# One pool of four two-bank PSUM tiles, and both halves of a block's bucket bits in one group, in a fused attention and channel-mix kernel

## The chip, the cores and the metric

The kernel runs on one core of one Trainium2 chip. Its measure is the device time in microseconds (us), the median of several executions. Executions of one kernel mostly agree within 1%. An execution more than 1.5% above the fastest of its kernel is called slow and is left out of every ratio.

## The reference, cut to what matters

```python
def _attn_ref(q, k, v, proj):                 # q, k, v: (4, 8, 768, 64); proj: (64, 6)
    q_bits = (np.einsum('bhsd,dk->bhsk', q, proj) > 0)
    k_bits = (np.einsum('bhsd,dk->bhsk', k, proj) > 0)
    # ... six bits make a bucket number ...
    mask = q_bucket[:, :, :, None] == k_bucket[:, :, None, :]
    scores = scale * np.matmul(q, k.transpose(0, 1, 3, 2))
    scores = np.where(mask, scores, -1000000000.0)
    # ... softmax ...
    return np.matmul(attn, v)

def _moe_ref(x, mu_k, mu_r, w_k, w_v, w_r):   # x: (4, 768, 512), heads side by side
    xk = mu_k * x + (1.0 - mu_k) * x_prev     # x_prev: x one row earlier
    xr = mu_r * x + (1.0 - mu_r) * x_prev
    k = np.maximum(xk @ w_k, 0.0)
    v = k * k @ w_v
    return 1.0 / (1.0 + np.exp(-(xr @ w_r))) * v
```

## The kernel before: the parts that matter

The kernel handles two heads at a time, as one of 16 blocks; four blocks make a batch, after which the "expert" matmuls (`w_k`, `w_r`, `w_v`) of that batch can run. The mask is built into the score matmul: each head's operands carry six extra rows with the signs of the projections. These signs come from the *bits* groups: matmuls on TensorE (PE), a VectorE (DVE) operation `bx` that reduces each result to a sign, and small copies into the operand's rows.

The program is recorded from a static plan. A list scheduler in the kernel file simulates the five engines with assumed durations and transfer times. At each free moment it takes the ready operation of lowest priority number (table `PR`). Then the instructions are recorded in exactly that order. On the chip every engine works through its own list in this order; semaphores, which the recording layer places, hold an instruction until what it depends on is done.

The kernel uses eight banks of PSUM, the memory that matmuls write to, of 512 fp32 columns each. Before, they were six tiles: two of two banks for score steps (1024 columns, read by one exp on ScalarE, ACT), and four of one bank for all small groups: bits, PV (the product of the exps with `v`), transposes, expert groups.

```python
    sc_t = [psum.tile([P, STEP], FP32, name=f"sc{i}", tag=f"sc{i}") for i in range(2)]
    sm_t = [psum.tile([P, 512], FP32, name=f"sm{i}", tag=f"sm{i}") for i in range(4)]
    plan = Plan({"sc": (2, 2), "sm": (4, 3)})     # slots; of them at most so many for expert groups
    # ...
    def sm(name):
        return sm_t[plan.slot[name]]
    # ... in add_bits, for each half h of the 768 columns:
            def f(nm=nm, h=h):
                ps = sm(nm)
                for w_, st in ((p1, True), (p2, False)):
                    for i in its:                 # q and k of both heads: four 32-row strips
                        a = side_a["qk"[i % 2]][sa]
                        nc.tensor.matmul(ps[32 * i : 32 * i + 32, 0:HALF], w_, a[:, i // 2, h * HALF : (h + 1) * HALF],
                                         start=st, stop=not st)
            def g(nm=nm, h=h):
                nc.vector.tensor_scalar(
                    out=bx_t[sx][lo_p:P, h * HALF : (h + 1) * HALF].bitcast(U16), # ...
                    scalar1=0x8000, scalar2=0x5400, op0=ALU.bitwise_and, op1=ALU.bitwise_or)
    # ... in the scheduler, when an operation takes a slot: the one that has been free longest
                    slot = avail[cls].pop(0)
```

The softmax here doesn't subtract the row's maximum and nothing guards it: scores larger than these inputs give would overflow.

Of the kernel before, what the change touches and what calls it, by code (L numbers as in the profile page):

```python
# [9 lines left out]
FP32 = mybir.dt.float32  # L10
FP16 = mybir.dt.float16
BF16 = mybir.dt.bfloat16
U16 = mybir.dt.uint16
AF = mybir.ActivationFunctionType
ALU = mybir.AluOpType
# [6 lines left out]


PR = {
    'ldq': -2.811, 'ldv': -2.337, 'hi': -5.393, 'lo': -1.084, 'tr': -2.122, 'bits': -1.224, 'bx': -4.393, 'row': 4.034,
    'va': 0.273, 'vsum': -2.003, 'mean': -0.515, 'pv0': 0.767, 'pv1': 1.128, 'fin': -1.916, 'ot': 1.215, 'xt': -1.326,
    'df': -1.607, 'xk': -3.487, 'xr': 2.133, 'moe': 4.97, 'mk': 2.095, 'mv': 2.279, 'sq': 0.189, 'os': 0.275,
    'tpe': -4.352, 'tev': -0.289, 'va_u': 2.059, 'vsum_u': -3.477, 'wk0': 38.237, 'wk1': 3.956, 'wr0': 54.984, 'wv0': 63.151,
    'wv1': -2.812, 'p0b': -9.506,
}  # L30


# [4 lines left out]
class Plan:  # L37
# [5 lines left out]



    def __init__(self, slots):
        self.ops = []
        self.writer = {}
        self.readers = {}
        self.slots = slots  # L50
        self.slot = {}

    def add(self, eng, dur, prio, fn, r=(), w=(), take=None, give=(), lag=None, name="", at=0.0, svc=0.0):
# [28 lines left out]
    def schedule(self):  # L82
        ops = self.ops
        engines = {"GQ": "POOL"}
        free = {e: 0.0 for e in ("PE", "ACT", "DVE", "POOL", "SP")}
        ready = {e: [] for e in free}
        avail = {c: list(range(n)) for c, (n, _) in self.slots.items()}
        moe_held = {c: 0 for c in self.slots}
        held = {}
        order = []  # L90
        events = [(o.at, 0, o.i) for o in ops]
        heapq.heapify(events)

        def met(i):
            o = ops[i]
            o.left -= 1
            if o.left == 0:
                heapq.heappush(ready[engines.get(o.eng, o.eng)], (o.prio, o.i))

        t = 0.0  # L100
        dma_free = 0.0
        while len(order) < len(ops):
            while events and events[0][0] <= t + 1e-9:
                _, kind, i = heapq.heappop(events)
                if kind == 0:
                    met(i)
                elif kind == 1:
                    o = ops[i]
                    for s in o.succ:
                        if ops[s].eng == o.eng and not o.svc:  # L110
                            met(s)
                elif kind == 2:
                    o = ops[i]
                    for s in o.succ:
                        if ops[s].eng != o.eng or o.svc:
                            met(s)
                    for name in o.give:
                        cls, slot, moe = held.pop(name)
                        avail[cls].append(slot)
                        moe_held[cls] -= moe  # L120
            progress = False
            for e in free:
                if free[e] > t + 1e-9:
                    continue
                skipped = []
                pick = None
                while ready[e]:
                    item = heapq.heappop(ready[e])
                    o = ops[item[1]]
                    if o.take is not None:  # L130
                        cls, name, moe = o.take
                        if not avail[cls] or (moe and moe_held[cls] >= self.slots[cls][1]):
                            skipped.append(item)
                            continue
                    if o.svc > 0.3 and o.prio > -9.0 and dma_free - t > BACKLOG:
                        skipped.append(item)
                        heapq.heappush(events, (dma_free - BACKLOG, 3, o.i))
                        continue
                    pick = o
                    break  # L140
                for item in skipped:
                    heapq.heappush(ready[e], item)
                if pick is None:
                    continue
                o = pick
                progress = True
                if o.take is not None:
                    cls, name, moe = o.take
                    slot = avail[cls].pop(0)
                    held[name] = (cls, slot, moe)  # L150
                    self.slot[name] = slot
                    moe_held[cls] += moe
                o.start = t
                free[e] = t + o.dur
                lag = o.lag
                if o.svc:
                    dma_free = max(t + o.dur + 0.9, dma_free) + o.svc
                    lag = max(lag, dma_free + 0.6 - t - o.dur)
                heapq.heappush(events, (t + o.dur + 0.1 * (o.eng in ("DVE", "ACT")), 1, o.i))
                o.vis = t + o.dur + lag  # L160
                heapq.heappush(events, (o.vis, 2, o.i))
                order.append(o)
            if not progress:
                if not events:
                    raise RuntimeError("the plan is stuck")
                t = max(t, events[0][0])
        self.end = max(o.start + o.dur for o in ops)
        return order
# [3 lines left out]
def kernel(  # L172
# [13 lines left out]
    nc = tc.nc  # L186

    B, H, S, D = q.shape
# [3 lines left out]
    P = 128  # L192
# [3 lines left out]
    HALF = S // 2  # L196
    STEP = 1024
# [26 lines left out]
    bx_t = [buf([P, S], FP16, f"bx{i}") for i in range(NBX)]  # L224
# [26 lines left out]
    p2 = buf([P, 32], FP16, "p2")  # L251
    muk = buf([P, NDC], FP32, "muk")
    mur = buf([P, NDC], FP32, "mur")
    sc_t = [psum.tile([P, STEP], FP32, name=f"sc{i}", tag=f"sc{i}") for i in range(2)]
    sm_t = [psum.tile([P, 512], FP32, name=f"sm{i}", tag=f"sm{i}") for i in range(4)]

    plan = Plan({"sc": (2, 2), "sm": (4, 3)})
    add = plan.add

    def sm(name):  # L260
        return sm_t[plan.slot[name]]

    DVE_C = lambda n, m=1.0: (n / m + 67) / 960.0
    ACT_C = lambda n: 0.068 + 0.833 * n / 1000.0
# [165 lines left out]
    def add_bits(n, heads):  # L430
        sa, sx = n % NAQ, n % NBX
        its = [2 * j + e for j in heads for e in range(2)]
        pb = n if n else PR["p0b"]
        lo_p = 64 * heads[0]
        for h in range(2):
            nm = f"bits{n}_{h}"

            def f(nm=nm, h=h):
                ps = sm(nm)
                for w_, st in ((p1, True), (p2, False)):  # L440
                    for i in its:
                        a = side_a["qk"[i % 2]][sa]
                        nc.tensor.matmul(ps[32 * i : 32 * i + 32, 0:HALF], w_, a[:, i // 2, h * HALF : (h + 1) * HALF],  # L443
                                         start=st, stop=not st)

            def g(nm=nm, h=h):
                nc.vector.tensor_scalar(  # L447
                    out=bx_t[sx][lo_p:P, h * HALF : (h + 1) * HALF].bitcast(U16),
                    in0=sm(nm)[lo_p:P, 0:HALF].bitcast(U16).rearrange("p (c e) -> p c e", e=2)[:, :, 1],
                    scalar1=0x8000, scalar2=0x5400, op0=ALU.bitwise_and, op1=ALU.bitwise_or)  # L450

            add("PE", 2 * MM(HALF) + 0.1, pb + PR["bits"], f, r=["p1", "p2"] + [("a", side, sa, j) for side in "qk" for j in heads],
                w=[(nm,)], take=("sm", nm, 0), name=nm)
            add("DVE", DVE_C(HALF), pb + PR["bx"], g, r=[(nm,)], w=[("bx", sx, h)], give=[nm], name=f"bx{n}")
        for i in its:
            side, j = "qk"[i % 2], i // 2

            def row(side=side, j=j, i=i):
                nc.sync.dma_start(out=side_a[side][sa][D : D + NB, j, :], in_=bx_t[sx][32 * i : 32 * i + NB, :])
            add("SP", 0.7, pb + PR["row"] + 0.01 * i, row, r=[("bx", sx, 0), ("bx", sx, 1)], w=[("ab", side, sa, j, h) for h in range(2)], svc=0.1, name=f"row{n}")  # L460

    def add_prep_first(n):
        s, sh, sa = n % NQ, n % NNH, n % NAQ
# [75 lines left out]
    def add_scores(n):  # L539
        sa, sp = n % NAQ, n % NPT  # L540
        for s in range(NSTEP):
# [4 lines left out]
            need += sorted({("ab", "k", sa, ch // NSC, (ch % NSC) // 3) for ch in chunks})  # L546

            def f(nm=nm, s=s):
                ps = sc_t[plan.slot[nm]]
                for lo, hi in pieces(s):  # L550
                    ch, q0 = divmod(lo, S)
                    j, jc = divmod(ch, NSC)
                    nc.tensor.matmul(ps[:, lo - s * STEP : hi - s * STEP], side_a["k"][sa][:, j, jc * P : (jc + 1) * P],  # L553
                                     side_a["q"][sa][:, j, q0 : q0 + hi - lo], start=True, stop=True)

            def g(nm=nm, s=s):
                nc.scalar.activation(out=pt_t[sp][:, s * STEP : (s + 1) * STEP], in_=sc_t[plan.slot[nm]],  # L557
                                     func=AF.Exp, bias=EBIAS, scale=ESC)

            T = n + s / NSTEP  # L560
# [187 lines left out]
```

## Time and profile before

| | |
|---|---|
| time, median of 3 | 258.73 us (258.31 to 258.94) |
| span in the profile | 256.8 us |
| PE / VectorE / ScalarE busy | 93% / 76% / 72% |

The head of the profile's page gives busy time, share of the span and number of instructions of each engine (PEld is PE's weight load):

```profile
span 256.8 us, 6319 instructions
## 1 busy us (share of the span) xinstructions
PE 239.3 (93%) x2519; PEld 143.5 (56%) x2519; DVE 195.1 (76%) x391; ACT 185.5 (72%) x242; POOL 57.9 (23%) x98
```

The table by stages gives, for each stretch of the span, each engine's busy us (number of instructions), then the granted PE clock, the DMA share and GB/s:

```profile
26.00:39.00 13.00, 12.04 (x188) 7.84 (x186) 9.07 (x18) 11.35 (x13) 4.11 (x7) 1.00 0.89 170
39.00:52.00 13.00, 10.92 (x155) 7.20 (x154) 9.52 (x18) 11.35 (x13) 2.85 (x7) 1.00 0.86 182
52.00:65.00 13.00, 11.04 (x149) 7.09 (x146) 9.80 (x18) 11.27 (x13) 7.60 (x13) 1.00 1.10 177
...
103.00:128.00 25.00, 25.00 (x303) 15.13 (x292) 23.05 (x44) 20.79 (x25) 6.48 (x8) 1.00 0.85 226
128.00:154.00 26.00, 24.90 (x283) 15.90 (x281) 24.50 (x52) 22.57 (x32) 8.63 (x11) 1.00 0.85 219
154.00:180.00 26.00, 26.00 (x274) 15.13 (x273) 23.52 (x43) 18.09 (x23) 5.64 (x8) 1.00 0.82 177
```

Before 65 us PE (first column of busy times) has gaps while ScalarE (fourth) is at 87%; later PE is full. The groups of instructions (busy us, mean ns of one, then idle time before them and its releaser):

```profile
L557 ACT ACTIVATE pt<-sc 128x1024 bf16<-128x1024 f32 x144 | 143.2, 1028 | 29.9 <-PE sc L553 28.3
...
L447 DVE TENSOR_SCALAR bx<-sm 128x384 uint16<-128x384 uint16 (+1 forms) x32 | 16.4, 549 | 3.3 <-PE sm L443 2.6
```

The table of waits (total us, times, longest) has these lines for the exps and scores, for the tanh of the `w_r` groups (`rs`), and for the multiply that follows it (`os`):

```profile
ACT pt L557 <- PE sc L553: 28.3, 48, 3.9
ACT rs L674 <- PE sm L671: 18.9, 13, 2.3
...
DVE os L688 <- PE sm L681: 16.4, 13, 2.1
...
PE sc L553 <- ACT pt L557: 4.5, 11, 0.7
```

Scores wait for a slot (last line), though only 4.5 us in all.

### The profile page before, as it was taken

Reading aid. Unit: us, or ns where it says so; the run is one execution under the profiler, and the core shown is the slowest. Engines: PE = TensorE matmul, PEld = TensorE weight load, DVE = VectorE, ACT = ScalarE, POOL = GpSimd, SP = SyncE. Lnnn points to the kernel's source line nnn. Section 1 sums busy time; section 2 is a strip of 40 time slices with the busy share of each in tenths; the row PEclk is TensorE's granted clock in tenths of the full one; section 3 lists DMA queues with packets and bytes.
Section 4 is the critical chain, followed back from the end, with each engine's and each line's share of the span. In section 5 each row is a group of like instructions: output and inputs, shape, how many; then the busy total and the mean of one; then the engine's idle time right before and its main releaser. Section 6 shows DMA issues by size and latency. Waiting matters only on the chain.

```text
span 256.8 us, 6319 instructions
## 1 busy us (share of the span) xinstructions
PE 239.3 (93%) x2519; PEld 143.5 (56%) x2519; DVE 195.1 (76%) x391; ACT 185.5 (72%) x242; POOL 57.9 (23%) x98
## 2 busy tenths in 40 slices
PE   6768898888999999999999989999999999999994
PEld 2334564555666456656666655555666666555441
DVE  4999676777789997989998999898685753675322
ACT  3838888888994598878898967586798986147320
POOL 2491415056051330504041424040000000000000
PEclk9998999999999999999999999999999999999999
DMA  6968979799998479796978987888200011220132
GB/s 191 382 168 155 163 174 172 199 171 180 225 201 227 116 199 175 212 241 190 274 148 266 216 241 149 233 164 166 89 3 6 3 41 43 82 86 1 41 123 82
DMA packets 64565, 39.78 MB, mean 155 GB/s; under 512 B 46756, under 2 KB 60952, under 8 KB 64536
## 3 DMA queue, kind: packets, MB, share of 16 engines
q1 hardware_dynamic: 62248, 36.76, 58.4%
q0 software_dynamic: 2208, 2.62, 6.3%
q8 instruction: 19, 0.31, 0.5%
q14 instruction: 10, 0.08, 0.1%
q10 hardware_dynamic: 80, 0.00, 0.0%
HBM read 24.12 MB, written 6.29 MB: 118 GB/s over the span
## 4 chain that ended last, share of the span: by engine, by line
PE 63%; DMA 15%; DVE 10%; POOL 3%; SPq 3%; issue 2%; ACT 2%; POOLq 0%; DVEq 0%
PE sc L553 16%; PE sm L681 15%; PE sm L652 11%; PE sm L583 10%; DMA vn<-in_v_dram 8%; PE sm L671 7%; PE sm L443 4%; DMA qn<-in_q_dram 3%; DMA ak<-kh 2%; POOL vt L360 2%; DMA kn<-in_k_dram 2%; PE sm L609 2%; ACT pt L557 2%; SPq L334 1%; DVE xk L635 1%
## 5 line engine op out<-in xcount | busy, mean ns | idle before, releaser
L557 ACT ACTIVATE pt<-sc 128x1024 bf16<-128x1024 f32 x144 | 143.2, 1028 | 29.9 <-PE sc L553 28.3
L553 PE MATMUL sc<-aq,ak 128*128 128x512 f16 (+1 forms) x384 | 84.6, 329 | 4.5 <-ACT pt L557 4.5
L553 PEld LDWEIGHTS <-ak 128*128 128x128 f16 x384 | 33.6, 98 | 31.1 <-issue 12.2
L652 PE MATMUL sm<-xk,wk 128*128 128x384 bf16 x256 | 48.9, 326 | 0.2
L681 PE MATMUL sm<-wv,k 128*128 128x512 bf16 x192 | 47.8, 379 | 1.1 <-DVE ob L599 1.1
L583 PEld LDWEIGHTS <-pt 128*128 128x128 bf16 x1152 | 42.9, 97 | 9.0 <-issue 0.6
L583 PE MATMUL sm<-va,pt 128*128 128x65 bf16 x1152 | 44.6, 193 | 0.0
L656 ACT ACTIVATE kr<-sm 128x384 bf16<-128x384 f32 x64 | 31.3, 498 | 9.5 <-PE sm L652 7.5
L652 PEld LDWEIGHTS <-wk 128*128 128x128 bf16 x256 | 24.1, 98 | 15.2 <-issue 0.3
L360 POOL TENSOR_TENSOR vt<-vn 128x384 f32<-128x384 f32 x12 | 15.1, 1256 | 71.5 <-DMA vn<-in_v_dram 71.5
L659 DVE TENSOR_TENSOR k<-kr 128x384 bf16<-128x384 bf16 x64 | 23.8, 385 | 8.5 <-ACT kr L656 8.4
L674 ACT ACTIVATE rs<-sm 128x512 f32<-128x512 f32 x24 | 14.4, 599 | 22.1 <-PE sm L671 18.9
L681 PEld LDWEIGHTS <-k 128*128 128x128 bf16 x192 | 18.4, 98 | 19.5 <-issue 1.3
L688 DVE SCALAR_TENSOR_TENSOR os<-rs,sm 128x512 f32<-128x512 f32 x24 | 16.3, 684 | 16.5 <-PE sm L681 16.4
L671 PE MATMUL sm<-wr,xr 128*128 128x512 bf16 x96 | 24.6, 379 | 0.0
L619 POOL COPY xt<-xt 128x127 bf16<-128x127 bf16 x16 | 8.4, 525 | 69.1 <-DVE xt L615 64.4
L447 DVE TENSOR_SCALAR bx<-sm 128x384 uint16<-128x384 uint16 (+1 forms) x32 | 16.4, 549 | 3.3 <-PE sm L443 2.6
L599 DVE TENSOR_TENSOR ob<-sm,rc 128x384 bf16<-128x384 f32 x32 | 17.8, 556 | 0.9
L405 DVE SCALAR_TENSOR_TENSOR kh<-kn,kh 128x768 f16<-128x768 f32 x15 | 18.3, 1219 | 0.1
L635 DVE SCALAR_TENSOR_TENSOR xk<-df,muk,xt 128x768 bf16<-128x768 bf16 x16 | 16.7, 1046 | 0.3
L443 PE MATMUL sm<-ak,p 128*32 128x384 f16 x124 | 14.4, 335 | 2.3 <-DVE ak L422 1.3
L635 DVE SCALAR_TENSOR_TENSOR xr<-df,mur,xt 128x768 bf16<-128x768 bf16 x16 | 16.1, 1018 | 0.0
(76 smaller groups left out, 195.3 us busy)
## 6 DMA issues: line engine op xcount, KB each, us to landing
vn<-in_v_dram SPq DMA_DIRECT2D x16, 384.0 KB
out_dram<-os SPq DMA_DIRECT2D x24, 256.0 KB
qn<-in_q_dram SPq DMA_DIRECT2D x15, 384.0 KB
kn<-in_k_dram SPq DMA_DIRECT2D x15, 384.0 KB
wk<-in_moe_w_k_dram POOLq DMA_DIRECT2D x4, 256.0 KB, 5.3
wv<-in_moe_w_v_dram POOLq DMA_DIRECT2D x4, 256.0 KB, 8.7
wr<-in_moe_w_r_dram POOLq DMA_DIRECT2D x2, 256.0 KB, 5.4
aq<-bx SPq DMA_DIRECT2D x31, 9.0 KB
```

The lines of the kernel that those rows point to most:

```text
L360: nc.gpsimd.tensor_tensor(out=vt[:, :, :, 0:E], in0=src[:, :, 0:3, 0:E], in1=src[:, :, 3:6, 0:E], op=ALU.add)
L405: nc.vector.scalar_tensor_tensor(out=nh[:, :, D:P], in0=nat.rearrange("p j (c d) -> p (j c) d", d=D), scalar=QS, in1=nh[:, :, 0:D], op0=AL ...
L443: nc.tensor.matmul(ps[32 * i : 32 * i + 32, 0:HALF], w_, a[:, i // 2, h * HALF : (h + 1) * HALF], start=st, stop=not st)
L553: nc.tensor.matmul(ps[:, lo - s * STEP : hi - s * STEP], side_a["k"][sa][:, j, jc * P : (jc + 1) * P], side_a["q"][sa][:, j, q0 : q0 + hi ...
L557: nc.scalar.activation(out=pt_t[sp][:, s * STEP : (s + 1) * STEP], in_=sc_t[plan.slot[nm]], func=AF.Exp, bias=EBIAS, scale=ESC)
L583: nc.tensor.matmul(oo[:, ic * 65 : ic * 65 + 65], pt_t[sp][:, o : o + P], va_t[sa][:, j, jc, 0 : D + 1], start=(not uc and ic == 0 and jc ...
L635: nc.vector.scalar_tensor_tensor(out=dst[smx], in0=df_t[sd], scalar=mu[:, t : t + 1], in1=x, op0=ALU.mult, op1=ALU.add)
L652: nc.tensor.matmul(ps[:, 0:HALF], wk_sb[:, d, fc * P : (fc + 1) * P], xk_t[mx[d]][:, h * HALF : (h + 1) * HALF], start=(d == 0), stop=(d = ...
L656: nc.scalar.activation(out=kr_t[sk], in_=sm(nm)[:, 0:HALF], func=AF.Relu, scale=0.5 ** 0.5)
L659: nc.vector.tensor_tensor(out=k2_t[s2][:, h * HALF : (h + 1) * HALF], in0=kr_t[sk], in1=kr_t[sk], op=ALU.mult)
L671: nc.tensor.matmul(sm(nr), xr_t[mx[d]][:, c * P : (c + 1) * P], wr_sb[:, d, :], start=(d == 0), stop=(d == NDC - 1))
L681: nc.tensor.matmul(sm(nv), k2_t[(b * NFC + fc) % NK2][:, c * P : (c + 1) * P], wv_sb[:, fc, :], start=(fc == 0), stop=(fc == NFC - 1))
```

## The change

All eight banks become one pool of four two-bank tiles. A score step takes a whole tile of the first three, when both banks are free; small groups take single banks, from bank 7 down to 4, so that they share banks 4 and 5 with the third score slot. The intent is a third score step in flight. The bits of both halves become one group of 768 columns, which takes a score slot, and one VectorE operation in place of two. All priorities are new as well.

```diff
 PR = {
-    'ldq': -2.811, 'ldv': -2.337, 'hi': -5.393, 'lo': -1.084, 'tr': -2.122, 'bits': -1.224, 'bx': -4.393, 'row': 4.034,
+    'ldq': -4.096, 'ldv': -2.786, 'hi': -4.393, 'lo': -1.809, 'tr': -9.712, 'bits': -6.189, 'bx': -3.768, 'row': 6.869,
     ... (all the other entries too)
+        def room(take):
+            cls, _, moe = take
+            if count[cls] >= self.most[cls] or (moe and count["moe"] >= self.moe_most):
+                return None
+            if cls == "sc":
+                for i in self.pairs:
+                    if not used[2 * i] and not used[2 * i + 1]:
+                        return i, (2 * i, 2 * i + 1)
+                return None
+            for b in self.banks:
+                if not used[b]:
+                    return b, (b,)
+            return None
     ...
-    sc_t = [psum.tile([P, STEP], FP32, name=f"sc{i}", tag=f"sc{i}") for i in range(2)]
-    sm_t = [psum.tile([P, 512], FP32, name=f"sm{i}", tag=f"sm{i}") for i in range(4)]
-    plan = Plan({"sc": (2, 2), "sm": (4, 3)})
+    ps_t = [psum.tile([P, STEP], FP32, name=f"ps{i}", tag=f"ps{i}") for i in range(4)]
+    plan = Plan((0, 1, 2), (7, 6, 5, 4), {"sc": 3, "sm": 4}, 3)
     def sm(name):
-        return sm_t[plan.slot[name]]
+        b_ = plan.slot[name]
+        return ps_t[b_ // 2][:, (b_ % 2) * 512 : (b_ % 2) * 512 + 512]
     ... (bits)
+            ps = ps_t[plan.slot[nm]]
+            for w_, st in ((p1, True), (p2, False)):
+                for lo, hi in ((0, 512), (512, S)):
                     for i in its:
-                        nc.tensor.matmul(ps[32 * i : 32 * i + 32, 0:HALF], w_, a[:, i // 2, h * HALF : (h + 1) * HALF], ...)
+                        nc.tensor.matmul(ps[32 * i : 32 * i + 32, lo:hi], w_, a[:, i // 2, lo:hi], start=st, stop=not st)
     ... (one tensor_scalar over ps[lo_p:P, 0:S] in place of two over 0:HALF)
-                w=[(nm,)], take=("sm", nm, 0), name=nm)
+            w=[(nm,)], take=("sc", nm, 0), name=nm)
```

## The prediction

> **What bounds the kernel now.** Two regimes. The table by stages shows TensorE (PE) busy throughout from 103 us to 231 us (24.90 of 26 us at worst), and the chain of waits there is almost all matmuls. Costing matmuls at the densest spacing in the timeline (a score step 0.44 us, a third of a PV group 0.38, four expert matmuls 0.65 or 0.86, a block's bits 0.76), I estimate 227 us of dense PE work in a span of 256.8. From 77 us the PE has no idle time worth naming until the last matmul at 253 us. The loss lies before 65 us, where I estimate only 44 us of dense PE work. There ScalarE sets the pace: from 26 to 65 us it runs 38 exp steps, although nine in a row took 8.72 us (0.97 each), so 40 would fit. From 13 to 26 us it runs 8 where 13 would fit; one wait is 3.86 us (second head's scores, behind its bits, the VectorE operation and the row copies).
>
> The groups show exp waiting for scores 28.3 us over 48 waits, scores for exp 4.5 us over 11. Most lie after 77 us and cost nothing. From 30 to 66 us they are 0.2-1.0 us each: with two score slots, every burst of PV, bits or transposes on the PE delays the refill. Such regular bubbles can mean that PSUM has run out (the Trainium skill, Perfetto Trace Analysis, "Optimization Strategy"); the trace agrees: score matmuls wait 0.32 us for an exp.
>
> **What the change does.**
> - A third score slot when two small banks are free, as they mostly are before 65 us. It lets exp run through a PE burst: I expect 2-3.5 us of ScalarE idle gone. In expert stages it is often missing; nothing is lost.
> - The bits group holds a score slot for about 2 us (matmuls, wait, VectorE): costs perhaps 0.5 us of the above.
> - Bits matmuls: 16 either way, same columns: still about 0.76 us a block.
> - VectorE: two operations of 549 ns become one of 768 columns. At 1.04 ns a column on about 150 ns fixed (from 549 at 384) that is 0.95 us: 0.15 us less a block, 2.3 us in all, perhaps 0.3 us of it critical at the start. Against it: it starts only after all 16 matmuls, so first bits matmul to row copies (1.6 us now) grows by 0.2-0.3 us. Nearly cancel.
> - New priorities (transposes of block 1 and bits earlier, xr far later) can move the start by 1-2 us either way; I count -0.5.
>
> A us saved on ScalarE before the PE saturates moves the end by one us; later, nothing. Sum: -3 to -3.5 us. The tail (expert matmuls from 228 us) stays.
>
> **Predicted: 255.4 us, 8 in 10 between 251.0 and 258.9.** Faster by over 2%: 0.24; within 2%: 0.70; slower: 0.06.
>
> **What would show it.** Right: 2-4 more exps before 65 us; most gaps of 0.2-0.6 us there gone; first expert matmuls 2-4 us earlier; PE full until 4 us before the end; the VectorE operation 0.95 us x16, its matmuls unchanged. Wrong: the same exp count by 65 us, or exp waiting while bits hold a slot.
>
> **What would make it wrong.** The start (before 26 us) improving by several us through the order, which would give over 2%; late xr stalling the r groups and emptying the PE; bits holding slots at bad moments.

## The result, and the profile after

| | before | after |
|---|---|---|
| time, median | 258.60 us (258.31 to 258.94) | 291.72 us (290.83 to 295.62) |
| ratio, 95% interval | | 1.1255 (1.1215 to 1.1295) |
| PE / VectorE / ScalarE busy | 93% / 76% / 72% | 86% / 67% / 64% |
| exp steps begun in the first 65 us | 45 | 40 |
| first expert matmul | 63.4 us | 68.9 us |

The change made the kernel 33 us slower. (The median before is now of four executions, one more than above.) The exps are counted once each, where they begin. The table by stages counts an exp that crosses a border in both stages; so the 38 exps that the prediction reads from it for 26 to 65 us are 35 that begin there, and there was more room than it says. The head of the page, the table by stages (the same columns as above), and the groups:

```profile
span 289.6 us, 6322 instructions
## 1 busy us (share of the span) xinstructions
PE 250.0 (86%) x2519; PEld 147.0 (51%) x2519; DVE 192.9 (67%) x375; ACT 184.8 (64%) x242; POOL 56.4 (19%) x98
```

```profile
26.00:39.00 13.00, 11.83 (x182) 7.63 (x181) 9.82 (x16) 11.20 (x12) 4.77 (x6) 1.00 0.82 131
39.00:52.00 13.00, 8.73 (x113) 5.81 (x110) 6.88 (x12) 8.96 (x10) 2.97 (x5) 0.91 0.68 164
52.00:65.00 13.00, 11.12 (x140) 7.45 (x139) 7.43 (x15) 9.61 (x11) 3.22 (x7) 0.83 0.87 143
...
103.00:128.00 25.00, 21.97 (x265) 12.92 (x264) 15.98 (x33) 14.32 (x16) 2.26 (x5) 1.00 0.74 171
128.00:154.00 26.00, 24.25 (x251) 14.52 (x253) 22.72 (x47) 19.42 (x27) 6.23 (x8) 1.00 0.70 171
154.00:180.00 26.00, 23.56 (x270) 14.23 (x262) 22.41 (x43) 18.90 (x25) 6.48 (x8) 1.00 0.81 203
```

```profile
L573 ACT ACTIVATE pt<-ps 128x1024 bf16<-128x1024 f32 x144 | 140.8, 1028 | 31.9 <-PE ps L569 31.3
...
L463 DVE TENSOR_SCALAR bx<-ps 128x768 uint16<-128x768 uint16 (+1 forms) x16 | 15.2, 952 | 6.5 <-PE ps L460 6.0
```

The work itself is as predicted: 2519 matmuls as before, exps of 1028 ns, and `bx` at 952 ns. What changed is that no engine is full any more in the stages where PE was full. The waits say for whom:

```profile
ACT pt L573 <- PE ps L569: 31.3, 34, 6.0
...
ACT rs L690 <- DVE os L704: 13.8, 6, 3.4
...
DVE os L704 <- PE ps L687: 11.1, 5, 3.7
...
PE ps L594 <- DVE rc L608: 3.7, 1, 3.7
...
PE ps L599 <- ACT kr L672: 2.1, 6, 0.6
```

Several of these are odd. Line 599 is PV, line 672 the relu of an expert group: PV reads nothing that relu writes, and the two use different banks. Line 704 multiplies `v` (line 697) by what tanh left, and here its wait is put down to line 687, the `w_r` matmuls, whose bank it does not read; before, VectorE waited at this multiply for the `v` matmuls alone (line 681 there). ScalarE's waits for VectorE add up to 22.4 us in this table (1.8 before), PE's for VectorE to 21.5 (7.4 before), VectorE's for PE to 58.4 (35.2 before).

The timeline (start us, us, instruction, idle time before it and its releaser) shows one case from the start, in the worst stretch of the first 65 us:

```profile
45.13 0.56 DVE L419 TENSOR_SCALAR qh<-qn 128x768 f16<-128x768 f32 x1
...
49.27 0.56 DVE L419 TENSOR_SCALAR kh<-kn 128x768 f16<-128x768 f32 x1 [3.58 <-DMA kn<-in_k_dram]
49.75 0.19 DVE L608 RECIPROCAL rc<-ps 128x6 f32<-128x6 f32 x1
...
49.99 0.48 PE L594 MATMUL ps<-vsu,tiny 128*128 128x390 bf16 x1 [3.74 <-DVE rc L608]
...
54.21 4.83 ACT L573 ACTIVATE pt<-ps 128x1024 bf16<-128x1024 f32 x5 [5.97 <-PE ps L569]
```

VectorE stands 3.58 us at an operation whose input, the load `kn`, has not landed. The next operations in its list, the reciprocal and the multiply of head 0's PV result, have to wait although their input is ready. PE then waits 3.74 us for that reciprocal, to start head 1's PV group in *another* bank, of the same two-bank tile. (The rebuilt program has it so: this matmul writes the first bank of tile `ps3`, and its wait names the reciprocal, which reads the second.) The exps run dry for 5.97 us. A standing PE also costs afterwards. Stages of 1 us show the granted clock (third number from the end):

```profile
49.00:50.00 1.00, 0.01 (x1) 0.01 (x1) 0.73 (x3) 0.00 (x0) 0.00 (x0) 0.78 0.20 69
50.00:51.00 1.00, 1.00 (x15) 0.82 (x15) 0.77 (x1) 0.00 (x0) 0.56 (x1) 0.50 0.00 0
...
55.00:56.00 1.00, 1.00 (x6) 0.54 (x5) 0.00 (x0) 1.00 (x2) 0.00 (x0) 0.50 1.02 172
56.00:57.00 1.00, 1.00 (x11) 0.79 (x9) 0.41 (x1) 1.00 (x2) 0.00 (x0) 0.80 1.17 247
```

Near the end of a stop of 3.7 us the clock falls to half, and it stays there from about 49.6 to 56.4 us. Before, it was at half only once while matmuls ran, for 3.4 us near 18 us. The Trainium skill says so too (TensorE: Matmul & The Clock Gate, "What's actually happening": half rate after an idle window of about 3.4 us, full rate after about as long busy); this trace agrees on the stop, and here the half rate lasted some 6.8 us, in which PE stood still in parts.

### The profile page after: what moved, and what is told of

Its sections match the earlier page's. It is cut to its first block, busy times and chain, and to the rows that moved or that the text cites. A ratio compares the mean times of both kernels' runs of the same rounds, so it can differ in the third digit from the quotient of the medians.

```text
span 289.6 us, 6322 instructions
## 1 busy us (share of the span) xinstructions
PE 250.0 (86%) x2519; PEld 147.0 (51%) x2519; DVE 192.9 (67%) x375; ACT 184.8 (64%) x242; POOL 56.4 (19%) x98
## 4 chain that ended last, share of the span: by engine, by line
PE 37%; DVE 6%; ACT 5%; DMA 3%; issue 2%; POOL 2%; SPq 0%; ACTq 0%; DVEq 0%; POOLq 0%
PE ps L697 10%; PE ps L668 10%; PE ps L569 6%; PE ps L599 6%; PE ps L687 4%; ACT kr L672 4%; DMA vn<-in_v_dram 3%; DVE os L704 1%; PE ps L460 1%; ACT rs L690 1%; DVE ob L615 1%; DVE va L402 1%; PE ps L625 1%; DVE xt L631 1%; POOL vt L377 1%
## 5 line engine op out<-in xcount | busy, mean ns | idle before, releaser
L573 ACT ACTIVATE pt<-ps 128x1024 bf16<-128x1024 f32 x144 | 140.8, 1028 | 31.9 <-PE ps L569 31.3
L569 PE MATMUL ps<-aq,ak 128*128 128x512 f16 (+1 forms) x384 | 82.4, 332 | 4.7 <-ACT pt L573 2.6
L599 PE MATMUL ps<-va,pt 128*128 128x65 bf16 x1152 | 48.3, 196 | 6.0 <-ACT kr L672 2.1
L668 PE MATMUL ps<-xk,wk 128*128 128x384 bf16 x256 | 49.2, 325 | 4.2 <-ACT kr L672 2.0
L697 PE MATMUL ps<-wv,k 128*128 128x512 bf16 x192 | 48.0, 378 | 4.9 <-DVE ob L615 2.4
L672 ACT ACTIVATE kr<-ps 128x384 bf16<-128x384 f32 x64 | 29.4, 493 | 30.4 <-PE ps L668 18.5
L704 DVE SCALAR_TENSOR_TENSOR os<-rs,ps 128x512 f32<-128x512 f32 x24 | 16.4, 682 | 20.4 <-PE ps L687 11.1
L687 PE MATMUL ps<-wr,xr 128*128 128x512 bf16 x96 | 24.6, 379 | 1.5 <-DVE os L704 1.0
L615 DVE TENSOR_TENSOR ob<-ps,rc 128x384 bf16<-128x384 f32 x32 | 17.8, 556 | 5.6 <-PE ps L599 2.4
L422 DVE SCALAR_TENSOR_TENSOR qh<-qn,qh 128x768 f16<-128x768 f32 x15 | 15.4, 1026 | 0.1
```

Source lines behind the costliest of these rows:

```text
L422: nc.vector.scalar_tensor_tensor(out=nh[:, :, D:P], in0=nat.rearrange("p j (c d) -> p (j c) d", d=D), scalar=QS, in1=nh[:, :, 0:D], op0=AL ...
L569: nc.tensor.matmul(ps[:, lo - s * STEP : hi - s * STEP], side_a["k"][sa][:, j, jc * P : (jc + 1) * P], side_a["q"][sa][:, j, q0 : q0 + hi ...
L573: nc.scalar.activation(out=pt_t[sp][:, s * STEP : (s + 1) * STEP], in_=ps_t[plan.slot[nm]], func=AF.Exp, bias=EBIAS, scale=ESC)
L599: nc.tensor.matmul(oo[:, ic * 65 : ic * 65 + 65], pt_t[sp][:, o : o + P], va_t[sa][:, j, jc, 0 : D + 1], start=(not uc and ic == 0 and jc ...
L615: nc.vector.tensor_tensor(out=ob_t[so][:, :, j * D : (j + 1) * D], in0=oo[:, :, 0:D], in1=rc_t[sr][:, 1, :].unsqueeze(2).to_broadcast([P, ...
L668: nc.tensor.matmul(ps[:, 0:HALF], wk_sb[:, d, fc * P : (fc + 1) * P], xk_t[mx[d]][:, h * HALF : (h + 1) * HALF], start=(d == 0), stop=(d = ...
```

## The experiments

Theory A: the recording layer keeps its waits per PSUM *tile*. Two small groups in the two halves of one tile are then taken to conflict, whatever their banks. Theory B: the tiles are innocent, and the new order is simply bad on the chip. Each kernel gave a correct result. "Before" was run again beside each set on the same chip, with medians of 258.4 to 260.5 us.

### Shared tiles

**e1_merged**: the kernel before, with its four one-bank tiles made halves of two tiles. Every engine's list was the same, instruction for instruction.

```diff
-    sm_t = [psum.tile([P, 512], FP32, name=f"sm{i}", tag=f"sm{i}") for i in range(4)]
+    sm2_t = [psum.tile([P, STEP], FP32, name=f"sm{i}", tag=f"sm{i}") for i in range(2)]
+    sm_t = [sm2_t[i // 2][:, (i % 2) * 512 : (i % 2) * 512 + 512] for i in range(4)]
```

> The kernel before, same instructions in the same order, but its four one-bank PSUM tiles are now halves of two two-bank tiles. Theory A (waits are kept per tile, so two small users that share a tile wait for each other although their banks differ): clearly slower, 275 to 300 us, with PV matmuls waiting for relu or ob of another group, and tanh waiting for os. Theory B (the new order and priorities are what is slow on the chip): 258 to 260 us, as before.

Measured: 285.85 us, ratio 1.105 (1.098 to 1.112). Comparing the two built programs, there are 269 places where an instruction of PE, VectorE or ScalarE waits for a later instruction of another of these engines than before, or waits for one where it had not waited. The waits of this run show the same odd pairs, a relu waiting for the `ob` multiply of PV, a tanh for the `bx` of bits:

```profile
ACT kr L657 <- DVE ob L600: 6.1, 7, 2.0
ACT rs L675 <- DVE os L689: 6.1, 3, 3.5
...
ACT rs L675 <- DVE bx L448: 4.0, 1, 4.0
```

ScalarE's waits for VectorE add up to 21.5 us. So the tile boundary alone, without third slot, new bits or new priorities, costs 26 us.

**e2_split67**: the changed kernel, same order, with banks 6 and 7 as tiles of their own.

```diff
-    ps_t = [psum.tile([P, STEP], ...) for i in range(4)]
+    ps_t = [psum.tile([P, STEP], ...) for i in range(3)]
+    top_t = {b_: psum.tile([P, 512], FP32, name=f"top{b_}", tag=f"top{b_}") for b_ in (6, 7)}
     def sm(name):
         b_ = plan.slot[name]
+        if b_ in top_t:
+            return top_t[b_]
```

> The changed kernel, same order, but banks 6 and 7 are two one-bank tiles; banks 4 and 5 still share one. Theory A: most of the loss comes back, 256 to 272 us. Theory B: still 288 to 295 us.

Measured: 273.36 us, 1.056 (1.049 to 1.063): 18 of the 33 us came back; ScalarE's waits for VectorE fell to 2.1 us. The timeline of this run at the same place as above:

```profile
45.90 0.33 PE L597 MATMUL top<-vsu,tiny 128*128 128x390 bf16 x1
...
49.58 0.56 DVE L422 TENSOR_SCALAR kh<-kn 128x768 f16<-128x768 f32 x1 [4.13 <-DMA kn<-in_k_dram]
50.06 0.19 DVE L611 RECIPROCAL rc<-top 128x6 f32<-128x6 f32 x1
...
53.50 0.82 PE L628 MATMUL top<-idb,ob 128*128 128x128 bf16 x6 [4.77 <-DVE ob L618]
```

VectorE again stands for the late load (4.13 us), but head 1's PV starts at 45.90 us and waits for nothing. PE stops later instead, at the transposes, which truly need VectorE's `ob`. That second stop belongs to the order and not to the tiles. Theory A is confirmed from both sides, though 273.36 us lies just above the range that I gave for it: 15 us are left.

**e3_nosib** (no tile has two small users: bank 4 is closed to small groups) and **e4_2slots** (two score slots, four one-bank tiles) take all sharing away.

```diff
 e3, on top of e2:
-    plan = Plan((0, 1, 2), (7, 6, 5, 4), {"sc": 3, "sm": 4}, 3)
+    plan = Plan((0, 1, 2), (7, 6, 5), {"sc": 3, "sm": 3}, 3)
 e4, on top of the changed kernel:
+    ps_t = [... for i in range(2)]
+    top_t = {b_: psum.tile([P, 512], ...) for b_ in (4, 5, 6, 7)}
+    plan = Plan((0, 1), (7, 6, 5, 4), {"sc": 2, "sm": 4}, 3)
```

> The changed kernel with banks 6 and 7 as one-bank tiles and bank 4 closed to small groups, so that no two small users ever share a tile; the third score slot stays, small slots are three. Theory A: all false waits gone; 252 to 262 us, unless three small slots are too few. Theory B: 280 us or more.

> The changed kernel with only two score slots and four one-bank tiles for small groups: the joint bits group (in a score slot) and the new priorities stay, the third slot and all sharing of tiles go. Theory A: 256 to 266 us, a little slower than before since bits take score slots. Theory B: 280 us or more.

Measured: 274.38 us, 1.058 (1.050 to 1.066), and 275.44 us, 1.065 (1.057 to 1.074). Neither range that I wrote for theory A held: with all tiles private 15 to 17 us remain. (Both runs are planned anew, so their order differs from that of the changed kernel.) A second cause exists.

### The order

Theory C: the rest is the order that the new priorities give. Theory D: it is the bits group in a score slot.

**e5_order_alone** is the kernel before with the new `PR` table. **e6_bits_alone** is e4, **e7_nosib_oldpr** is e3 and **e8_split67_oldpr** is e2, each with the old `PR` table.

```diff
 PR = {                                   # e5, in the kernel before; the rest alike
-    'ldq': -2.811, 'ldv': -2.337, 'hi': -5.393, 'lo': -1.084, 'tr': -2.122, ...
+    'ldq': -4.096, 'ldv': -2.786, 'hi': -4.393, 'lo': -1.809, 'tr': -9.712, ...
 PR = {                                   # e6, e7, e8, in the kernels of e4, e3, e2
-    'ldq': -4.096, 'ldv': -2.786, 'hi': -4.393, 'lo': -1.809, 'tr': -9.712, ...
+    'ldq': -2.811, 'ldv': -2.337, 'hi': -5.393, 'lo': -1.084, 'tr': -2.122, ...
```

> The kernel before with the new priorities and nothing else. The 14 us that stay with no shared tiles come either from the order that the new priorities give (theory C: 266 to 280 us here) or from the bits group in a score slot (theory D: 257 to 262 us here).

> Two score slots, four one-bank tiles, the joint bits group in a score slot, and the old priorities. Theory C (order): 257 to 263 us. Theory D (bits in a score slot): 268 to 278 us.

> Three score slots, no tile with two small users, joint bits, and the old priorities. Theory C: 253 to 262 us; if the third slot is worth the 2 to 3.5 us of my prediction, 255 to 257. Theory D: 265 us or more.

> As the changed kernel with banks 6 and 7 as one-bank tiles (banks 4 and 5 shared), with the old priorities. Theory C: 254 to 264 us, perhaps some us above the kernel without any sharing. Theory D: 268 us or more.

Measured: e5 267.18 us, 1.038 (1.032 to 1.044); e6 275.46 us, 1.066 (1.061 to 1.072); e7 271.35 us, 1.052 (1.046 to 1.057); e8 268.77 us, 1.041 (1.037 to 1.045). The new priorities alone cost 9 us in the old layout, but going back to the old ones does not repair the new layout. e5 fell into the range of theory C, and e6, e7 and e8 into those of theory D, so neither C nor D alone fits; e12 below speaks against D. A changed layout makes the scheduler produce another order even with the old priorities, so I asked what *any* other order costs.

**e9_jitter_a**, **e10_jitter_b**, **e11_jitter_c**: the kernel before, each of 28 priorities of the engines (the texts below say 29, a miscount) moved up or down by 0.1 (two draws) or 0.25, for example

```diff
-    'ldq': -2.811, 'ldv': -2.337, 'hi': -5.393, 'lo': -1.084, 'tr': -2.122, 'bits': -1.224, 'bx': -4.393, 'row': 4.034,
+    'ldq': -2.911, 'ldv': -2.437, 'hi': -5.293, 'lo': -1.184, 'tr': -2.022, 'bits': -1.124, 'bx': -4.293, 'row': 4.134,
```

> The kernel before with each of its 29 engine priorities moved by 0.1 up or down at random, nothing else: a control for any change of order. Theory F (the old priorities fit the old order on this chip, and any other order costs): 262 to 272 us. Theory G (what costs is in the parts of the change themselves, not in the mere change of order): 257 to 261 us.

> The same control with other random signs. Theory F: 262 to 272 us. Theory G: 257 to 261 us.

> The same control with steps of 0.25. Theory F: 264 to 275 us, more than with 0.1. Theory G: 257 to 262 us.

**e12_third_alone**: the kernel of e7 with the bits again in two small groups.

```diff
-        nm = f"bits{n}"
-        ... (one group over two banks, take=("sc", nm, 0), one VectorE operation)
+        for h in range(2):
+            nm = f"bits{n}_{h}"
+            ... (the old code: take=("sm", nm, 0), one VectorE operation for each half)
```

> Three score slots and three small ones, no tile with two small users, the bits in two small groups as before, old priorities: the third slot alone. Theory F: 262 to 272 us, like any new order. Theory G with the joint bits as the cost: 254 to 260 us, well under the 271 of the same with joint bits.

Measured: e9 268.87 us, 1.036 (1.030 to 1.041); e10 263.62 us, 1.015 (1.010 to 1.020); e11 267.62 us, 1.029 (1.025 to 1.032); e12 276.55 us, 1.068 (1.060 to 1.075). All three control runs are slower than the old order: 4 to 9 us for a change that means nothing. (The larger step did not cost more, as I had expected.) The old priorities seem to fit one order on this chip. e5's 9 us are about what a random nudge costs. e12 has no joint bits and is slower than e7, above both of its ranges. By the ratios the joint bits did not cost in that layout but saved 4 us; or e12's order was the worse one, which this pair cannot tell.

### The third slot and the choice of bank, at a kept order

**e13_first_free**: the kernel before, same lists, but the lowest free slot is taken. **e14_bits_rotate** and **e15_split67_rotate**: e6 and e8, same lists, but the bank free longest is taken (in e15 of banks 6 and 7 first), and of the score slots too.

```diff
 e13: the kernel before
-                    slot = avail[cls].pop(0)
+                    slot = min(avail[cls]); avail[cls].remove(slot)
 e14, e15: room() of the changed kernel
-            for b in self.banks:
+            for b in sorted(self.banks, key=lambda b: (b not in (4, 5, 6, 7), freed[b])):     # e15: (6, 7)
```

> The kernel before, same order of instructions on every engine, but a small group takes the lowest free bank, as the changed kernel does, in place of the one that has been free longest. Theory H (taking the bank that was freed last removes the slack that the plan's errors need): 261 to 268 us. If H is wrong: 258 to 260 us.

> The run with two slots, joint bits and old priorities (275.5 us), same order, but each group takes the bank that has been free longest. Theory H: 266 to 271 us, 5 us or more come back. If H is wrong: 273 to 277 us, and the order alone explains it.

> The run with banks 6 and 7 as own tiles and old priorities (268.8 us), same order, but banks 6 and 7 taken in turn. Theory H: 262 to 266 us. If H is wrong: 267 to 270 us.

Measured: 259.74 us, 1.002 (0.995 to 1.009); 273.27 us, 1.052 (1.043 to 1.060); 269.98 us, 1.044 (1.036 to 1.053). My theory H, that reusing the bank freed last takes away slack, falls: e13 and e15 show nothing, and e14 went from 1.066 to 1.052, short of the 5 us or more expected.

**e16_third_order_kept**: the kernel before with exactly its lists. From the middle of block 0 to the first expert group, while at most two small groups live, two of the four small banks are one two-bank tile, the third score slot, and small groups keep the other two as tiles of their own. Before and after that the four are as they were.

```diff
     order = plan.schedule()
+    # live[w]: small groups alive at place w; swap1, swap2: the stretch in which at most two are
+    # slots are given out again along the finished order: a third score slot inside the stretch
     with tc.manual_schedule():
-        for o in order:
+        for w, o in enumerate(order):
+            if w in (swap1, swap2):
+                top.close()                       # two one-bank tiles <-> one two-bank tile
+                ...
             o.fn()
```

> The kernel before, with exactly its order of instructions on every engine; between the start and the first expert group (while at most two small groups live) scores have a third two-bank tile of their own and small groups two banks; before and after that the old four. If the third slot is worth what I predicted: 254 to 257 us. If exps have little to gain at a fixed order: 257.5 to 259.5 us. If the slot itself costs, as the runs with a new plan might suggest: 262 us or more.

Measured over fast runs: ratio 0.9998 (0.992 to 1.007); the median of all six, three of them slow, is 261.33 us against 260.45. In the built program some 40 waits of PE for ScalarE come earlier or go, some 20 of PE for VectorE come later or are new, and 14 of the 144 score steps take the third slot. The slot neither costs nor gains anything that the fast runs could see. They are only half of e16's executions, against 8 of 11 before; over all executions the means are 261.4 us and 260.0. The kept trace is a slow one, so no trace shows the slot in a fast run. In it scores waited for an exp once, 0.2 us (11 times, 4.5 us, before): the waits that the slot was to remove went, and no gain followed. The expected 254 to 257 us are ruled out in part only: the interval allows a gain of up to 0.8%, 2 us, and as much loss.

### What makes an order bad

In the fronts of e2, e5, e6, e7 and e8 PE or VectorE waits 2 to 6 us near 50 us for a load or another transfer. In e5 to e8 three or four expert-weight loads had gone out between 39 and 45 us, where in the kernel before only two did. (In e2, as in the changed kernel, only two had, and the wait for `kn` came all the same.) The bits group of e6 is such a case:

```profile
40.85 2.14 POOL L331 DMA_DIRECT2D wk<-in_moe_w_k_dram  x3
...
50.14 0.58 PE L461 MATMUL ps<-ak,p 128*32 128x512 f16 x1 [4.64 <-DMA ak<-kh]
```

**e17_wk_later**: e6, with three weight loads sent out later. **e18_wk_sooner**: the kernel before, with its third and fourth sent out earlier. All other lists are kept.

```diff
     order = plan.schedule()                             # e17, in the kernel of e6
+    gq = [o for o in order if o.eng == "GQ"]            # the ten weight loads
+    order = [o for o in order if o not in gq[:3]]
+    at = order.index(gq[3])
+    order[at:at] = gq[:3]
     order = plan.schedule()                             # e18, in the kernel before
+    gq = [o for o in order if o.eng == "GQ"]
+    order = [o for o in order if o not in gq[2:4]]
+    at = order.index(gq[1]) + 1
+    order[at:at] = gq[2:4]
```

> The run with two slots, joint bits and old priorities, where three weight loads went out at 40.9 us and the bits matmuls then waited 4.6 us for a transpose (51.5 us). Same order on PE, VectorE, ScalarE and the load queue; only these three weight loads go out later, beside the fourth at about 57 us. Theory I (the orders of the new plans collide on the DMA where the plan did not expect it, and every engine then stands in its place): 268 to 272 us, that wait under 1.5 us. If not: 273 to 277 us.

> The kernel before with its third and fourth weight loads sent out at about 41 us, with the first two, in place of 53.5 and 54.4 us; all else in the same order. Theory I: a wait of 2 us or more for a load or a transpose appears on PE or VectorE between 45 and 55 us, and the time is 261 to 266 us. If not: 258 to 260 us.

Measured: e17 275.88 us, 1.063 (1.058 to 1.068); e18 262.68 us, 1.014 (1.009 to 1.019). In e18 the collision came as expected, and with it 4 us, in the kernel that was good (there the first of these waits was 1.62 us):

```profile
39.60 2.31 POOL L313 DMA_DIRECT2D wk<-in_moe_w_k_dram  x4
...
47.72 0.56 DVE L402 TENSOR_SCALAR qh<-qn 128x768 f16<-128x768 f32 x1 [2.48 <-DMA qn<-in_q_dram]
...
51.28 0.56 DVE L402 TENSOR_SCALAR kh<-kn 128x768 f16<-128x768 f32 x1 [2.01 <-DMA ak<-bx]
...
52.37 0.82 PE L609 MATMUL sm<-idb,ob 128*128 128x128 bf16 x6 [2.48 <-DVE ob L599]
```

In e17 the wait at 50 us went (10 exps began between 39 and 52 us, where e6 had 7), but the loads now went out at 52.7 us and the same kind of wait came 19 us later:

```profile
52.67 2.32 POOL L331 DMA_DIRECT2D wk<-in_moe_w_k_dram  x4
...
69.42 0.58 PE L461 MATMUL ps<-ak,p 128*32 128x512 f16 x1 [5.05 <-DMA ak<-kh]
```

The time did not fall. So colliding transfers in a fixed order do cost (e18), but e6's wait seems only to have moved, and e17 does not show how much of e6's 17 us they are.

## Why the prediction was wrong, point by point

| step of the prediction | what the runs showed |
|---|---|
| two regimes, PE full from 77 us, ScalarE pacing before | not contradicted; that slots can win time in the first one is not shown (e16) |
| "A third score slot ... I expect 2-3.5 us of ScalarE idle gone" | at a kept order 0.9998 (0.992 to 1.007): between 2 us gained and 2 us lost |
| "In expert stages it is often missing; nothing is lost" | **the step that failed first**: the layout that brings it puts two small groups in one tile; this alone costs 26 us in the old order (e1), and undoing most of it returns 18 us in the new (e2) |
| "The bits group holds a score slot ...: costs perhaps 0.5 us" | scores waited 3.2 and 4.7 us for `bx` in the two-slot layouts (e6, e4), 1.1 us in the changed kernel; its effect on the time stays open |
| bits matmuls 0.76 us a block, `bx` 0.95 us | right: the same 16 matmuls spread over 0.83 us of the timeline where nothing comes between, before and after; `bx` took 952 ns |
| "New priorities ... I count -0.5" | **mis-sized**: +9 us alone (e5); random nudges of 0.1 to 0.25 cost 4 to 9 us (e9 to e11) |
| 2-4 more exps before 65 us, first expert matmuls 2-4 us earlier | 5 fewer (40 against 45), 5.5 us later |

The step that failed is the description of the third slot. I priced a slot as a bank that is free or not. I did not ask at what grain the waits are kept when two groups lie in one tile. The diff shows it: `sm()` stopped returning a whole tile and began to return half of one. The Trainium skill (PSUM — Partial Sum Buffer, "PSUM bank collisions raise a hardware error") asks for semaphores by bank and quadrant, so two banks need no mutual wait, and the kernel before was correct without any; the program had them all the same, 269 in e1, since the layer that places semaphores went by tiles. A prediction from the code could have counted them: each place where two small groups of one tile live at once ties PE, ScalarE and VectorE to each other's slowest step.

The mechanism is a chain. In a static order VectorE stands in place for a load. With private tiles PE goes on until it needs VectorE's own result. With shared tiles PE and ScalarE stop at once, at an instruction that only shares the tile (49.99 us above); in one stop PE fell to half clock.

Of the 33 us, then, 18 to 26 are the shared tiles (shown from both sides). The rest is 4.1% to 6.8%, 11 to 18 us, in every kernel with the new slots and few or no shared tiles that was planned anew. I attribute it to orders that do not fit the chip, which is argued and not shown: shown is that each of the four other orders of the old kernel that were run costs 4 to 10 us (e5, e9 to e11), and that one provoked collision of loads costs 4. Why the new layouts' orders cost more than random nudges, and how much of it is the bits group in a score slot (which I could not test at a kept order, since the old lists leave no two-bank slot for it), stays open. No version that I ran beats the kernel before.

The VectorE saving was right by size (two of 549 ns against one of 952 ns). From the two durations, a column costs (952 - 549) / 384 = 1.05 ns and an operation 146 ns besides; the Trainium skill (VectorE: DVE Perf Modes, "The TRN2 errata") gives a measured fixed term of about 150 cycles of a 0.96 GHz clock, by estimate 156 ns, for another form of operation: near, and the trace decides. The prediction's split into 1.04 ns a column and 150 ns could not be read from one size alone; the second size bears it out. But VectorE did not bound the kernel, and the 2.3 us saved (16 times 146 ns) did not show in its time.

## What to carry to other kernels

Before you merge buffers into larger tiles, ask at which grain the waits are kept; if it is the tile, a half of a tile is not a free slot, and building the old kernel with only the tile boundary moved tells you at once (the order stays, the waits change, the time shows it). In a kernel whose order comes from such priorities, measure first what a meaningless nudge costs; here 4 to 9 us, more than the gain that the change was after. An engine's list in a fixed order passes every late transfer on, so look for what stands in the list behind it, and not only for the late transfer.

## What the Trainium skill lacked or had wrong

- PSUM — Partial Sum Buffer: its rule is to guard by bank; no page says that a two-bank tile used as two slots gets waits between its halves. The runs show what that costs: 258.7 to 285.9 us with the same order (e1).
- Perfetto Trace Analysis, "Optimization Strategy": regular bubbles can mean that PSUM has run out. Here score matmuls did wait for an exp (11 times, 4.5 us in all), and a third slot at the same order gave 0.9998 (0.992 to 1.007). The hint was no measure of a gain.
- Perfetto Trace Analysis, "Optimizing Tensor Performance": independent groups should rotate through different banks. Taking the lowest free bank, which still moves on while one is in use, in place of the one free longest gave 1.002 (0.995 to 1.009) in this kernel (e13), so that choice did not matter here.
- No page speaks of how far a static order chosen for one layout loses its worth when anything moves: 1.5% to 3.6% for random nudges of the priorities (e9 to e11).
